# Constants fetched to one partition and spread by a matmul, with a new order table, in a fused attention and rational feed-forward kernel

## Chip, cores and metric

The kernel runs on one core of one Trainium2 chip. The metric is the device time of one launch in microseconds (us), the median of three runs: 771.01 us before the change (770.82 to 772.5).

## What is computed

Two small attentions in a row, then a feed-forward layer whose activation is a quotient of polynomials. B = 8 batches, H = 8 heads, 576 rows of 64, 32 packed rows; d_model 512, d_ff 2048. The weights w_in and w_out, a and b arrive as float64 words or float32 as the host gives them; the two weights are fetched as 64-bit words and turned into float32 on the chip.

```python
def sm_attn(qq, kk, vv):
    s = scale * np.matmul(qq, kk.transpose(0, 1, 3, 2))
    s = s - np.max(s, axis=-1, keepdims=True)
    a = np.exp(s)
    a = a / (np.sum(a, axis=-1, keepdims=True) + 1e-09)
    return np.matmul(a, vv)
p_packed = sm_attn(p, k, v)
out = sm_attn(q, p_packed, p_packed)
...
h = x @ w_in
P = a[0] + a[1] * h + a[2] * h2 + a[3] * h3
Q = 1.0 + np.abs(b[0]) * np.abs(h) + np.abs(b[1]) * h2
g = P / (Q + 1e-6)
return (g @ w_out).astype(np.float32)
```

## The kernel before

**How the work is cut.** The feed-forward layer is cut into 128 units (batch, half of its 576 rows, chunk of 256 of the 2048 columns), 16 to a batch (lines 976 to 980). A unit makes its h by matmuls into the PSUM banks h (TensorE, `hidden`, L902), reads it three times on ScalarE (Y, U and sq, lines 918 to 920), works on Y on VectorE (921, 922), adds U and sq on GpSimd, takes logarithm and exponential on ScalarE and finishes g on VectorE (929 to 941). Three units later `acc_block` (L983) multiplies g by the w_out chunk into the banks acc. The first 12 units are computed in plain float32; after them every operand is split in a high and a low part and three products stand for one.

**Ahead of the units** stands the attention of batch 0 (`attention`, L636): keys (tiles nat0 and nat1, and their last 64 rows in AH) are transposed by TensorE, scored against p, turned by softmax on ScalarE and VectorE and multiplied by v into ppT; then the queries (tile w3) are transposed, multiplied by ppT, and a second softmax on VectorE (lines 849 to 865) leaves AH, the left operand of every h of the batch. The attention of each later batch is fed in between the units.

**Weights.** `load_words` (L466) fetches a chunk of w_in or w_out (1 MB as 64-bit words, two DMAs of 512 KB); `convert` (L517) turns it into float32 with two passes on ScalarE, two on VectorE and an addition on VectorE or GpSimd. Sixteen chunks in all.

**Constants.** `constants` (L423) makes a tile zero on VectorE, fetches a and b by two DMAs that repeat them on all 128 partitions (tile ab, lines 425 and 426), scales them into abS (427), works out a square root in eleven small instructions on the tile root (432 to 443) and loads four of the scaled values into ScalarE's registers (444, 445), which the three reads of h use as scale.

**What sets the order.** No instruction is issued where it is written. `Planner` (L106) records every operation; `order` (L287) decodes the text ORDER into one permutation of all recorded operations, and `issue` (L303) hands them to the engines in that permutation. Each engine's queue is therefore fixed, and worked off in order: an instruction whose operand is late holds up all behind it. SyncE issues every DMA but two, and in the trace the ones it issues use eight semaphores in turn. The planner's own costs (COST, DMA_RATE, `transfer`, `replay`) set nothing at run time but one thing: `idle` (L1110) puts filler matmuls, ident times zero, issued at L310, where the planner sees TensorE empty.

```python
low, high = np.frombuffer(zlib.decompress(base64.b85decode(ORDER)), np.uint8).reshape(2, -1).astype(int)
order = (np.cumsum(low + 256 * high) % 2**16).tolist()
...
for i in self.order():
    engine, calls = self.ops[i]
```

In the views of the profile nearly all instructions carry line 313, where `issue` calls the engine, so tiles tell them apart, not lines.

Of the kernel before, what the change touches and what calls it, by code (L numbers as in the profile page):

```python
# [13 lines left out]
F32 = mybir.dt.float32  # L14
# [5 lines left out]
ALU = mybir.AluOpType  # L20
# [17 lines left out]
    "j^%sxFC96&svVfn@4DY1LWY9Ht)($bs(yIUz6E`9PpfSCYjE3{ir)Wv%o3*5%N@wntuGI^ezGzZZT;D!%Le>6?_c+MMaAdQhS7>O"
    "ZxPxbZz<?wiyT9Cccrhn{@SHRk=x&*gf23>^mI+Gw?=%WLG=0E?O88T@6NvSfV3L=D}%3W*s@=KwMmovqOf<T$o9dUORZlHuM3oj"
    "2144Z5qomq8-ILw+txQEs(UV7`S1VOxJP$R(bN;yefQmxQ0j&6EO3QN6CsmqbpB0$#k1esVaw`+mi*=&`Ip{0YfIx{HMq=4&8S`>"  # L40
    "+VQXjXFTF0PU^3G>vLbwl&=fQHvR7I9ZbDz>!+jAu8k+m-u+w7Z0yZYq91<fO%>E-gF0|2BoDl!Nab^xI(PWdx8-f8#R^g4sVC-+"
    "d2Ol{XM99R_sDiN9#8)Ck0nkmEjKMcQV79)?`Q12=Wn^`VnUtMDLqzZ;ZeIIqP_Ktidev<%Tc-VYjRnb%9iy0{h_RG)gf^qT;?{5"
    ";*GsaKO;u1l(W%tfypj9D-CUXUXu*1a7inVv|Wppg=^H^LA40ijT$pXqMORnnz{A6^97mDn!INZ@o&4u?cX~T+xk@H@<XCWccqd_"
    "DmnL}R5GSa;|cug&B^DU)F!jqtxxKn`lTT*e)9Jz(BM&K%Z`W~4-o|-6{Vi|1%by*5qj|tUcZ{t$ew*6@%%4{`~GO7rSG2EcHg_3"
    "-k@?C_s4fq5oMCZ-&*(4_q<R4w#-9N;FZR<ti79p4Zo`fvZHcL24GMpmBW(ku3rqK-ZVZH5504*RGHj)Z$&ahyta86w5N@#ggirQ"
    "0|x3^9Rz>=dS7iw7onc{&DbA)?UldsqCB3Ze*9|ORXe1Wdtv*L)2`CCV^#3LizL7goF{02KqbV~sk9bPhvlG1r7bDaW1+QiB2xI("
    "i|$vRt997DF%y8_NTKWxLiK4g1!z^dVxT%4%j&dFbx=mBq6KY|0=E_L+M^4IPESotJy;bd0JKr-HHXADYr!r^nw3KeOPF5Ksj?rt"
    "jrmd^UvV^DA8$NZ<~1w(OB@#KWlOy$mAdWSd(PJMr<Yv}mDV}0Et8&yaEU11`r$WDWJ>XbYTn71rM1Irj%r+$WW-SyYQLE__tn;Q"
    "j4c^%K`*XSLpGTj(v>RuAW)?q1$u7MtrVM8fw2nl07;CfEih<Sffx7Gc}gjd9UNDi8oct1+dh_)>Vsg>xTI$22^c_?0F5OWva35="
    "sH3xBpc?P2lbh4Sj@6!|zg){il1d|*2JKa31R!?PKWcU9g-80=^jV<(Y|4z-&AGhq$QpexUDIE4q}Blbv})gaA|6u%49|<F^$;+8"  # L50
    "u@Jd!z>pI4FOmj&mcsE(r-zqj<la(%baxd6Uo<PUgSsS{W5~g(G^0SCmIWh~;IV{s@~&ClDzACiDvuM$_pa~n3f7KVH4c+v$*Hj%"
    "nb58HJ6VWX(&=jdaK+6B%mG74M@A?((5CA(=pYl*lO5GzP{*8)bO2n?SVC)eD^yg!g=pTp;lSO8v&-67eOwV|M6}j>E4;bJVW%5h"
    "CF+k2Cm-$!RirW`M5HYa-IY1R$(H^^W`2}@Z?h~r7LjT7QfI-ATzhrH{)&6INmj};zNfYh*TdR(4fO0WgM3Wk0__uT4w8|(V0U$V"
    "$==FtjViMKvlU(L)%*29m6U>?A3UO+_pt@sF})>I?|ki{*@w!q{&M8Ij67mWr<LWG<_wv_4}PE=uwFCj!vFFIrDfge%W?}0&qlH9"
    "wE{ZW@V2+p%0fcjGaFW!caiHpqGif?f3JiPU5OA%${A7G<fEi0Qo)Qhr9n%N*}@d0k|tIMduLJTLu{-rh$7{;sp*^{sPD0n;5CPJ"
    "jL2(7X#rY5sRv}l<TF9Kpae(`R15<&Tmdy`X{#F`RIa=VTD7%zR&S^+q|=>6N!sw%TI=p_p3F<CV0^gqn|@DFF9O<{L=X&H(luvG"
    "%KF+4SX<AKLpm~Z`+iX!oLg|Y5n0uoRso>oI=A5TTt%v<E%zl_VGeCR+je%2=wkWE+>6a!^MXSQ(>P?QPgemPz8!qs%a5)o>C}ac"
    "pZqK1`eZd^OZ;$fd07ZK2?_oNwJ55AKYcGJ4eQXELJRu<jxF<CUFIPhM8ii`=8ml_6^&$NP%4Hu9=Uq#E}+7&XX7#CB=1Iz<bx*G"
    "1BV|k`v|R;moyDmKxYeF(Shk2WwL%=XYDY9A?i)pwKS-@D<N*VR2^#>>|c#s?CQK@p!!SSonI1h@14$@E_5~9uBzuT7fQ~T5LJFT"
# [36 lines left out]
    "eyTH=Kn8hX7jOnAvjw9Bl!<Xuc2WkXqQI3xhFf^?Sec6+j^~)Eij5m(VE{3vD9?&c!wC3-D;wMrj}Z_!#$y1!Uh-fyojR;`O{&<q"
    "h6ziZsRhSN4{jxi6_JsE#JJg897|48O!NFq@Dh?9#&=k;Blu+xN6du`z^n3jmhyzKs5rrRQo{&GPeExKH^uTNjK5IaxhW)65y7#A"
# [1066 lines left out]
```

## Time and profile before

| | |
|---|---|
| time, median of 3 runs | 771.01 us (770.82 to 772.5) |
| span of the profiled execution, first to last instruction | 770.6 us |
| median less span | 0.4 us |
| TensorE busy | 742.8 us, 96% of the span |
| VectorE busy | 683.9 us, 89% |
| ScalarE busy | 654.6 us, 85% |
| GpSimd busy | 470.5 us, 61% |
| moved by DMA | 56.04 MB |

Engines are named PE (matmul), PEld (weight load), DVE (VectorE), ACT (ScalarE), POOL (GpSimd) and SP (SyncE). A busy PE can hide waits, because matmuls are pipelined and their ends are modelled. The filler matmuls count as busy too.

### The profile page before, as it was taken

What the parts mean: (1) busy time and instruction counts of PE and PEld (TensorE: products, weight loads), DVE (VectorE), ACT (ScalarE), POOL (GpSimd) and SP (SyncE); (2) the same over time, 40 slices, a digit from 0 to 9 for tenths busy, and PEclk for the clock granted to TensorE, in tenths of its full rate; (3) what the DMA queues carried; (4) which work ended last, traced back from release to release, by engine and by line L of the source; (5) the groups of instructions that cost most, each with busy time, mean ns of one, the idle gap of its engine ahead of it and who ended that gap; (6) DMA issues with size and microseconds to landing.
All of it is one profiled execution on the core that took longest, in us unless ns stands there. A gap on an engine that the chain in (4) does not pass through costs nothing.

```text
span 770.6 us, 15197 instructions
## 1 busy us (share of the span) xinstructions
PE 742.8 (96%) x5440; PEld 572.8 (74%) x5440; DVE 683.9 (89%) x1290; ACT 654.6 (85%) x1465; POOL 470.5 (61%) x456
## 2 busy tenths in 40 slices
PE   1899999999999999999999999999999999999997
PEld 1665544688787887788788887778788887878886
DVE  4799999998998889998999889998999889989873
ACT  4799998999887898889887898889887898898973
POOL 1134468866685556756685556755686556866653
PEclk9999999999999999999999999999999999999999
DMA  9994630206501155024601165023801131000001
GB/s 283 301 344 163 188 47 1 86 29 70 90 1 55 46 69 90 1 87 57 103 1 55 46 68 92 2 86 42 117 1 55 42 56 37 1 29 1 27 2 42
DMA packets 152044, 56.04 MB, mean 73 GB/s; under 512 B 122144, under 2 KB 141344, under 8 KB 151968
## 3 DMA queue, kind: packets, MB, share of 16 engines
q1 hardware_dynamic: 151744, 54.81, 31.9%
q8 instruction: 43, 0.70, 0.4%
q14 instruction: 33, 0.27, 0.1%
q10 hardware_dynamic: 224, 0.26, 0.1%
HBM read 45.62 MB, written 9.44 MB: 71 GB/s over the span
## 4 chain that ended last, share of the span: by engine, by line
PE 81%; DVE 6%; DMA 5%; ACT 5%; SPq 1%; POOL 1%; issue 1%; DVEq 0%; POOLq 0%; ACTq 0%
PE acc L313 42%; PE h L313 24%; PE at L313 14%; DVE Y L313 3%; DMA m<-in_moe_w_in_dram 2%; DMA w<-in_q_dram 1%; SPq L313 1%; ACT Y L313 1%; ACT sq L313 1%; DMA out_dram<-half 1%; POOL gl L313 1%; ACT U L313 1%; DMA w<-in_moe_w_in_dram 1%; DVE small L313 1%; DVE V L313 1%
## 5 line engine op out<-in xcount | busy, mean ns | idle before, releaser
L313 PE MATMUL acc<-w,gh 128*128 128x512 f32 x732 | 238.5, 407 | 0.7 <-ACT half L313 0.3
L313 POOL TENSOR_TENSOR U<-U,sq 128x576 f32<-128x576 f32 x128 | 184.3, 1440 | 88.5 <-ACT U L313 38.6
L313 PE MATMUL h<-AH,m 128*128 128x288 f32 x1024 | 201.8, 314 | 2.7 <-DVE Y L313 2.4
L313 PEld LDWEIGHTS h<-AH,m 128*128 128x128 f32 x1024 | 161.4, 188 | 42.3 <-DVE Y L313 21.0
L313 POOL TENSOR_TENSOR gl<-Y,gh 128x512 fp32r<-128x512 f32 x116 | 150.3, 1296 | 48.5 <-ACT gh L313 19.0
L313 PEld LDWEIGHTS acc<-w,gh 128*128 128x128 f32 x732 | 132.0, 188 | 40.1 <-issue 10.2
L313 ACT ACTIVATE Y<-h,abS 128x288 f32<-128x288 f32 x256 | 127.0, 511 | 31.0 <-PE h L313 24.0
L313 PE MATMUL acc<-w,gl 128*128 128x512 f32 x382 | 148.5, 413 | 0.0
L313 DVE SCALAR_TENSOR_TENSOR Y<-Y,abS,V 128x576 f32<-128x576 f32 x128 | 103.0, 805 | 32.9 <-ACT V L313 32.4
L313 ACT ACTIVATE sq<-h 128x288 f32<-128x288 f32 x256 | 106.9, 419 | 27.7 <-PE h L313 16.0
L313 DVE TENSOR_TENSOR Y<-Y,h 128x288 f32<-128x288 f32 x256 | 110.9, 446 | 21.2 <-ACT sq L313 6.0
L313 DVE SCALAR_TENSOR_TENSOR Y<-Y,abS,h 128x288 f32<-128x288 f32 x256 | 125.7, 505 | 2.6
L313 ACT ACTIVATE U<-h 128x288 f32<-128x288 f32 x256 | 101.9, 422 | 8.2 <-DVE V L313 6.2
L313 ACT ACTIVATE V<-U,one 128x576 f32<-128x576 f32 x128 | 98.3, 768 | 6.6 <-DVE Y L313 4.1
L313 PE MATMUL h<-AL,m 128*128 128x288 f32 x448 | 97.9, 295 | 0.0
L313 DVE SCALAR_TENSOR_TENSOR V<-U,V 128x576 f32<-128x576 f32 x128 | 96.2, 752 | 0.0
L313 DVE SCALAR_TENSOR_TENSOR Y<-V,Y 128x576 f32<-128x576 f32 x116 | 87.0, 750 | 1.5
L313 PEld LDWEIGHTS acc<-w,gl 128*128 128x128 f32 x382 | 71.4, 188 | 21.3 <-issue 7.7
L313 ACT ACTIVATE V<-V 128x576 f32<-128x576 f32 x128 | 84.2, 658 | 1.1
L313 PE MATMUL acc<-half,gh 128*128 128x512 f32 x240 | 80.7, 411 | 0.0
L313 ACT CAST gh<-Y 128x512 fp32r<-128x512 f32 x116 | 73.6, 634 | 6.2 <-DVE Y L313 5.7
L313 PEld LDWEIGHTS h<-AL,m 128*128 128x128 f32 x448 | 72.8, 188 | 0.9
(146 smaller groups left out, 973.8 us busy)
## 6 DMA issues: line engine op xcount, KB each, us to landing
w<-in_moe_w_out_dram SPq DMA_DIRECT2D x16, 512.0 KB, 5.7
out_dram<-half SPq DMA_DIRECT2D x15, 512.0 KB, 3.0
nat<-in_k_dram SPq DMA_DIRECT2D x48, 144.0 KB, 3.9
nat<-in_q_dram SPq DMA_DIRECT2D x48, 144.0 KB, 4.3
nat<-in_v_dram SPq DMA_DIRECT2D x24, 256.0 KB, 3.2
m<-in_moe_w_in_dram SPq DMA_DIRECT2D x10, 512.0 KB, 7.6
w<-in_moe_w_in_dram SPq DMA_DIRECT2D x6, 512.0 KB, 8.6
nat<-in_k_dram SPq DMA_DIRECT2D x4, 512.0 KB, 6.6
```

The source lines that it names most:

```text
L313: getattr(getattr(self.nc, engine), name)(*args, **kwargs)
```

## The change

The constants come to one partition (tile row, two DMAs with one row each) and are spread to all 128 by a matmul of a row of ones with them, into the bank V, from which VectorE copies ab. Tile zero and the ones are made ahead of the planned part. The planner's costs are altered, and the order table is another one.

```diff
-    DMA_ISSUE, DMA_START, DMA_END = 420, 1400, 1200
-    DMA_RATE = 100.0, 190.0, 370.0
+    DMA_ISSUE, DMA_START, DMA_END = 420, 1500, 2000
+    DMA_RATES = (4096, 395.0), (2048, 345.0), (1024, 308.0), (512, 270.0), (256, 225.0), (0, 100.0)
...
         if engine == "vector" and name == "tensor_scalar":
             per /= 2
+            fixed += (self.columns(aps[0]) == 128) * 64
+        if engine == "vector" and name == "reciprocal" and self.columns(aps[0]) > 8:
+            fixed += 83
+        if engine == "scalar" and name == "activation" and aps[0].space == aps[1].space == PSUM:
+            fixed += 25
...
+    tc.nc.vector.tensor_scalar(zero, ident[:, 0:D], 0.0, None, ALU.mult)
+    ones, row = sb.tile([1, P], F32, name="ones"), sb.tile([1, 6], F32, name="row")
+    tc.nc.vector.memset(ones, 1.0)
...
     def constants():
-        nc.vector.tensor_scalar(zero, ident[:, 0:D], 0.0, None, ALU.mult)
-        nc.sync.dma_start(ab[:, 0:4], a.rearrange("(o n) -> o n", o=1).broadcast_to([P, 4]))
-        nc.sync.dma_start(ab[:, 4:6], b.rearrange("(o n) -> o n", o=1).broadcast_to([P, 2]))
+        nc.sync.dma_start(row[:, 0:4], a.rearrange("(o n) -> o n", o=1))
+        nc.sync.dma_start(row[:, 4:6], b.rearrange("(o n) -> o n", o=1))
+        t = V_ring.next()[:, 0, 0:6]
+        nc.tensor.matmul(t, ones, row, start=True, stop=True)
+        nc.vector.tensor_copy(ab, t)
```

The two order tables, decoded, differ in these places (m0 to m3 are the first four chunks of w_in; places count from 0 on each engine's own queue):

| queue | before | after |
|---|---|---|
| SP, the first 28 DMAs | m0, m0, m1, m1, last keys, m2, m2, p four times, keys nat0, keys nat1, last queries twice, m3, m3, last v twice, v, v, w_out, w_out, queries, queries, b, a, last keys of batch 1 | keys nat0, last queries, a, b, last keys, last queries, m1, m1, p, m0, p, p, p, m0, m2, m2, keys nat1, m3, m3, v, v, w_out, last v twice, w_out, queries, queries, last queries of batch 1 |
| SP, next | w_out into w2, w_out into w3 (after the queries), keys of batch 1 | w_out into w2, keys of batch 1, w_out into w3 |
| VectorE, the twelve instructions on abS and root (427 to 443 but the memset) | places 29 to 57, the last seven of them inside the second softmax | places 1 to 21 |
| ScalarE, first entry | conversion of m0 | register load from abS |
| TensorE, the first entries | 16 transposes of nat0 and nat1, then p and the last keys | transposes of nat0 mixed with the new matmul, the last keys and p, then those of nat1 |
| VectorE, last instruction but one or two of unit 0, 1, 2, ... 7 (L930) | 76, 88, 104, 114, 134, 145, 155, 167 | 72, 86, 104, 121, 135, 145, 153, 166 |
| ScalarE, exponential of unit 0, 1, ... 7 (L928) | 68, 80, 95, 108, 123, 136, 149, 166 | 64, 78, 94, 109, 124, 137, 149, 167 |

All bytes fetched up to the second transfer of the queries are the same in both: 16 DMAs of 512 KB, one of 128, four of 64 and four of 16, so 8640 KB (8.85 MB), and the constants after the change. On each engine the entries differ until what ran at 337 us in the trace before (SP 199 us, GpSimd 371 us); behind that the queues are the same.

## Rows read from the trace of the kernel before

**Rows 1.** The page: busy time of the matmul engine, DVE, ACT and POOL, and the busy share of PE in 40 slices of 19.3 us.
```profile
PE 742.8 (96%) x5440; PEld 572.8 (74%) x5440; DVE 683.9 (89%) x1290; ACT 654.6 (85%) x1465; POOL 470.5 (61%) x456
PE   1899999999999999999999999999999999999997
```

**Rows 2.** Busy time by stretch: the stretch and its length in us, then busy us and instructions of PE, PEld, DVE, ACT and POOL, the granted clock of PE, the share of the DMA engines' time and GB/s. The last row is the filler matmuls of L310 alone (PE and PEld), from 0 to 60 us.
```profile
0.00:16.00 16.00, 0.00 (x0) 0.00 (x0) 5.33 (x7) 7.05 (x7) 1.29 (x8) 1.00 0.90 280
16.00:32.00 16.00, 14.24 (x204) 11.60 (x204) 11.77 (x22) 12.34 (x25) 4.50 (x2) 1.00 1.06 315
32.00:44.00 12.00, 10.75 (x147) 7.33 (x147) 11.61 (x31) 8.45 (x18) 0.00 (x0) 1.00 0.90 292
44.00:60.00 16.00, 14.90 (x120) 10.12 (x121) 14.54 (x25) 15.94 (x34) 8.52 (x5) 1.00 1.07 351
60.00:90.00 30.00, 28.96 (x206) 15.72 (x205) 29.53 (x60) 29.03 (x60) 12.94 (x8) 1.00 0.49 165
90.00:110.00 20.00, 20.00 (x129) 10.46 (x127) 19.14 (x31) 19.90 (x45) 11.95 (x8) 1.00 0.55 96
110.00:250.00 140.00, 140.00 (x928) 102.87 (x928) 130.91 (x248) 121.70 (x269) 102.04 (x96) 1.00 0.24 46
250.00:338.00 88.00, 87.63 (x709) 69.78 (x703) 82.46 (x161) 78.05 (x182) 55.93 (x58) 1.00 0.30 52
338.00:740.00 402.00, 400.12 (x2891) 323.03 (x2890) 363.17 (x683) 348.44 (x804) 258.68 (x260) 1.00 0.26 47
740.00:771.00 31.00, 26.16 (x130) 21.88 (x128) 15.45 (x27) 13.66 (x30) 14.65 (x15) 1.00 0.08 26
...
0.00:60.00 60.00, 13.16 (x118) 10.15 (x118) 1.00 0.99 310
```

**Rows 3.** The chain of work that ended last, from 0 to 60 us: start, length, what. A DMA's piece goes from its issue to its landing.
```profile
4.28 10.09 DMA m<-in_moe_w_in_dram
...
21.64 10.22 DMA w<-in_q_dram
31.86 0.14 issue
```

**Rows 4.** What reads the constants: the tile root and its instructions (shortest, median and longest ns, first and last start in us), and of the tile ab how long DVE sat idle for its two DMAs and how long these took from issue to landing.
```profile
L313 DVE TENSOR_SCALAR root<-root x5: 112/149/266, 33.7 to 39.5; 128x1 int32<-128x1 int32 x3, 128x1 f32<-128x1 f32 x2
L313 DVE RECIPROCAL root<-root x2: 154/154/154, 38.7 to 42.0; 128x1 f32<-128x1 f32 x2
L313 DVE SCALAR_TENSOR_TENSOR root<-root x1: 213/213/213, 42.2 to 42.2; 128x1 f32<-128x1 f32 x1
L313 DVE TENSOR_SCALAR abS<-root x1: 155/155/155, 42.5 to 42.5; 128x1 f32<-128x1 f32 x1
...
  DMA ab<-in_moe_b_dram: 0.6, 1
  DMA ab<-in_moe_a_dram: 0.2, 1
...
DMA to landing us min/median/max: 8.1/9.1/10.1
```

**Rows 5.** DVE in order of time: start, length, instruction, and in brackets the idle time ahead of it and who ended it.
```profile
35.06 0.47 DVE L313 STREAM_TRANSPOSE kx<-at 128x288 f32<-128x288 f32 x1
...
38.69 0.15 DVE L313 RECIPROCAL root<-root 128x1 f32<-128x1 f32 x1
38.79 0.75 DVE L313 TENSOR_REDUCE small<-kx 128x18 f32<-128x576 f32 x1
39.46 0.27 DVE L313 TENSOR_SCALAR root<-root 128x1 f32<-128x1 f32 x1
39.64 0.17 DVE L313 TENSOR_SCALAR small<-small 128x18 f32<-128x18 f32 x1
...
43.32 1.43 DVE L313 STREAM_TRANSPOSE AH<-kx 128x576 f32<-128x576 f32 x2
...
48.88 0.45 DVE L313 TENSOR_TENSOR Y<-Y,h 128x288 f32<-128x288 f32 x1 [0.50 <-ACT Y L313]
51.45 1.14 DVE L313 TENSOR_SCALAR w<-w 128x1024 int32<-128x1024 int32 x1 [0.66 <-ACT win L313]
```

**Rows 6.** PE in order of time: the first transposes, the transposes of the last queries, the product of the queries with ppT, the first h and the first product with w_out.
```profile
16.40 1.09 PE L313 MATMUL at<-ident,nat 128*128 128x128 f32 x4 [16.40 <-DMA nat<-in_k_dram]
17.28 1.91 PE L313 MATMUL acc<-ident,nat 128*128 128x128 f32 x8
...
32.65 0.98 PE L313 MATMUL acc<-ident,w 128*128 128x128 f32 x7
...
34.03 0.71 PE L313 MATMUL at<-kx,ppT 64*32 64x288 f32 x16
...
44.15 2.21 PE L313 MATMUL h<-AH,m 128*128 128x288 f32 x8 [0.21 <-DVE AH L313]
...
59.19 2.74 PE L313 MATMUL acc<-w,gh 128*128 128x512 f32 x6
```

**Rows 7.** ACT: the copy that leaves ppT.
```profile
31.43 0.37 ACT L313 COPY ppT<-acc 128x256 f32<-128x256 f32 x1 [0.41 <-PE acc L313]
```

**Rows 8.** Who PE waited for between 90 and 740 us: us in total, times, longest.
```profile
PE h L313 <- DVE Y L313: 1.7, 3, 0.7
```

More of the change, by code (lines that the diff above doesn't have):

```diff
@@ L38 @@
[L38 to L47, printed above, removed]
@@ L98 @@
[L98 to L102 removed]
+    "c-rk*XP6u1wVtC@*Nob#Yo+bY+uYU-_ue43!A>9$0|^EjE+LSR<R&2y$n^z697r7OKp=roOaME?xL{)&_kz8)xA$FbkydR~M!n4a"
@@ new lines @@
+    "v@Sa{TArJGpZv&=cvo7LZ{|DYJ@0$YXFNv+BT@?Zbt$+w$*FDCLe5CB*aO36C_b=^_QRzqc<91sxBY!hLO2tiyn~jBfc$V%$-s+}"
+    "HM&>6zBl~RQ{f%QtJ07Z#^{%R8i)32KY32nQg&|dFS^P)tCBg%1*abWjf|!*OpWlq{k||=(s%D`;s~XRi|_rjM=o+d{x-N?cw^<Z"
+    "J1@6s79BC)`I0Kl_ezqycn(ka`u&@?=S1LpJGE&D;2|ZXbKthNPM)W}pRQ=F=zRFZF^xlC*I0dE?U%xd7arU;skio`FtO+z<4Zr9"
+    "Te@?RWWniAR=4)Rs@UrfKKyEG=x_I&&D#=e>@A9SY<j2uxF%dDgwny|b9lj%x6$+`YZJmly#IO>c~l`51qv>j?{4Gm(F%pZIXU#6"
+    ")qgh)t^H)}t$(7e2d5tVW@_K2kp<g(RAridYTA6?cK@yXkIiBK3|m30+dso_K0^ENTKVY#UajN37aJxQ{NAWHH>~b$(S<`3yUL8i"
@@ new lines @@
+    "u|ct=`mMEbQGfOBg{N1#k1e|DTX=Zh9j^??yqnyOb@PrliY>w~v^8^|S%2I<L)bTzSI<8r*z(5GJKsH=SWfTteDLDdJA}Vo{h0Yx"
+    "-Sk~5WqtQN`vraeFV~k-o&ra}GfV$P<+`o&|ElBV%-EwjTRP#sm!uQz&uo0+<B`bBwt8MpS5aHBFp&<*?tNz6Zb8N2X*T=9A1vR@"
+    "+dF8a1*><=?d_;1C>~j!R!Ewv+-Y}l=hh=l3gN8uUR+Bx{qoIxCk_way#&(20iBRX5<R>^%ly3|{G@p08*}e^?<Y@G?4N$5uHtW{"
+    "55Mo#YAM~N&Bt7m8&1w~DW^9l(-T{(=WkdU!mSOn9lnik2@}Nnza)xheL&Y=%zyXgw~Kj>#8mt=;e{Xnije90WRBOLcwoOTw@*#S"
+    "@A*r9t12=1gevjpg9oS$$5-qdR8xkKKqOkw+9F6Q6JQO5NedZLY3!=0Z6S*Au0QE9Ywc0OUm6LgMf4r-`4(Olr0R~El8MOujeV<j"
@@ new lines @@
+    "8?M&XPk3Gin%Io?GldJzQc6nHW>y&8Nx$Vkf0hj7MYNAT{Lr!Q{#1&G2);+|!e!Ktwi+g$O9^*A693K{DJrE;np?!hSKs-?eLE~I"
+    ")+e741r&n!mmXX$_o>1JX^g*nU#Pf&ugKrJ+6)kQbVo$}f#=7zd>H=w2K7$f?%yl=C*AgLidyoUTjHXxPkNS!N`ezE#Kf{4k4S9!"
+    "(cf+shy#^hRyEwxU9$c|aC})Ti%s)6j1H-zlK9K5jtakE0L1a%KDT@QkDnvDgxfZkhk4F;sp*c7x}EWLXJ;<>usf#PyhAEozeCei"
+    ">IRKx`*X>kKdtEd-D5h@<J<f$5p3I{4Q_iprjdXDuV-cfT>ag&!k&ven_vD>X!{o3o-0p-yQ&8V!}dFbgGPQ{Aefs7ntMK8E0ObL"
+    "aZykXbM`ytJoa))_i=Ojcd(@#zWY<Z@~LMviXQNmdRyjheMp<|?)-_z6bJIv2Xk~)8=f6pykWEI#b1x)XgBYub-0GMZg;1i*$kKO"
@@ L103 @@
+    "tWo1DB?|lJNfiD6m#BX$)IU+7=zmP3*sborkV0Wx$Ymvf9!GH5T{NdWIia9g>$1Yd>1eYCsjMPnvlsX1G#eJ#QxeTQp~@P4xCap&"
+    "$Ho;#I;&}+S?6h-6T+;zVm92|(<qvCI>fG??AdXg<5#Ym7{;33m}jnBv8S1{?szRfXDDVhHFVZ&HFjv6)dsOhWIXv{&>aU{<Di!z"
+    "zN`b??9()EP0@7L=`sBkn4>ZJE8?Fma2UqrOV)8fHW{-Sjpibbv6!n?jH7whNW(frW#ob80*4->Mb1fN)-e?KjDlInS$!sFSmicF"
+    "*(#4=Sq)S6*+y24bGu(`9I?$l72)XkI3340QOB~6gXpXQc%1)S$#xOL#-{_8Qy8~H{2xDA<Y)"
 )
@@ L186, in transfer @@
         size = mybir.dt.size(args[1].dtype)
-        run = 1
-        for step, n in reversed(args[1].ap):
-            if step != run:
-                break
-            run *= n
+        runs = []
+        for dims in (args[1].ap, args[0].ap[1:]):
+            run = 1
+            for step, n in reversed(dims):
+                if step != run:
+                    break
+                run *= n
+            runs.append(run * size)
         n = 1
@@ L194, in transfer @@
             n *= m
-        return n * size / self.DMA_RATE[(run * size >= 256) + (run * size >= 1024)]
+        return n * size / next(rate for least, rate in self.DMA_RATES if min(runs) >= least)
     def price(self, engine, calls):
```

125 lines of the change are left out of this document (65 added, 60 removed).

## The prediction

> **What bounds the kernel now.** I read the busy shares first. TensorE (PE) is busy 96% of the span and its 40 slices are full but for the first and the last [rows 1], so whatever the change does must show in the time in which PE has nothing useful to do. The table by stretch says where that is [rows 2]. PE is busy 0 of the first 16 us, 14.24 of the next 16, 10.75 of 12 and 14.90 of 16: 39.9 of 60 us. Of these, 13.2 us are fillers, so up to 60 us PE works for 26.7 us and loses 33.3. From 60 to 90 us it loses 1.0, from 90 to 740 us 2.3 us (0.37 between 250 and 338, 1.88 behind it), at the end 4.8. What the change can win lies ahead of 90 us, therefore, and every us won there is a us of the total only if PE's dense part starts that much earlier.
>
> Who holds PE up there? Three limits follow each other. Up to 32 us it is the transfers: the DMA engines are at 0.90 and 1.06 of their time while VectorE (DVE) is busy 5.33 of 16 and 11.77 of 16 us, and the chain that ended last goes through transfers to the landing of the last queries at 21.64 + 10.22 = 31.86 us [rows 3]. From 32 to 44 us it is DVE, 11.61 of 12 us: scores come at 34.03 + 0.71 = 34.7 us, DVE's second softmax runs from 35.06 to 43.32 + 1.43 = 44.75 us, and the first h follows at 44.15 us, beside the second half of the last transpose [rows 5, 6]. From 44 to 90 us DVE (44.1 of 46) and ScalarE (ACT, 45.0 of 46) are both full: the chunks are converted on the same engines that work on the units, and the first product with w_out comes at 59.19 us only [rows 2, 6]. From 90 us on it is PE.
>
> **The change part by part.** All terms are changes of the profiled execution, whose span is 770.6 us; the median of the runs is 771.0, so 0.4 us lie around the span, and I carry them along.
>
> *Keys ahead.* The first keys can be transposed at some 5 instead of 16 us. But the bytes up to the last queries are the same 8.85 MB in both orders. They landed within 31.9 us, and ppT, which the early keys serve, was ready at 31.43 + 0.37 = 31.8 us [rows 7], while the queries' own transposes, which land after it, run to 32.65 + 0.98 = 33.6 us [rows 6]. Keys that come earlier shorten a branch that the queries end anyway; moreover the second keys stand behind 4.0 MB in the new order, behind 3.87 MB in the old, so the first scores cannot start before them. Gain 0. Cover: the landing of the queries. If it were gone, the most to be had is ppT's lead on the product of the queries, 34.0 less 31.8 = 2.2 us.
>
> *The constants' way.* The two repeated fetches landed 8.1 and 10.1 us after their issue, behind the queries, and DVE sat idle 0.6 + 0.2 us for them [rows 4]. That idle time was not the limit: the conversion it held up ended before the scores came. Now they stand third and fourth on SyncE's queue, ahead of everything that they delay. Their price on the queries' landing is bounded by 0 and by what they took at the end of the queue, two landings 0.3 us apart behind 31.86 (22.06 + 10.1 and 24.38 + 8.1 give 32.2 and 32.5); with one row for 128 I take 0.1 in all. The added matmul and copy have no row; the nearest are a small instruction of DVE, 0.15 us [rows 4], and a transpose, 1.09 / 4 = 0.27 us [rows 6]. They fall where PE had no work and DVE a third of its time, so 0. ACT's queue now begins with a register load that waits for them, and the conversions behind it start later; ACT was busy 7.05 of the first 16 us, and the landings of the first chunks hold it up. 0, and 1 us at most.
>
> *Root out of the softmax.* Seven instructions of DVE on root and abS stood between 35.06 and 43.32 us, in the very chain that gives AH. By their durations [rows 4] they are 0.11, 0.15, 0.27, 2 x 0.154, 0.21 and 0.155: 1.2 us at most. But neighbours overlap: from a root instruction to the next one it is 38.69 to 38.79 and 39.46 to 39.64, so 0.10 and 0.18 us for durations of 0.15 and 0.27 [rows 5]. Six of the seven are nearer to the short one: 6 x 0.10 + 0.18 = 0.8 us. I take 0.8, and 0.2 more since the transpose that started at 35.06 can follow the scores of 34.7. AH comes 1.0 us earlier (0.6 to 1.5). What is late next is the conversion of w_out chunks, as before.
>
> *Order from 32 to 60 us.* The DMA share fell to 0.90 between 32 and 44 us, 1.07 behind it: 0.17 x 12 = 2 us of transfer time were lost where SyncE waited for the queries to be transposed before it could refill their tile. The new order puts 512 KB of keys ahead of that wait, so that the chunks behind land 1 to 2 us earlier. DVE waited 0.66 us for a conversion and 0.50 us for the first Y [rows 5]; against this ACT does one more pass of a conversion ahead of the first Y; the nearest row is such a pass on DVE, 1.14 us [rows 5]. So between +1.1 and -1.2, the two waits together; I take -0.4, as the lost transfers speak for the gain.
>
> *Order from 60 to 90 us.* By their places, the last DVE instructions of units 0 to 7 come 4, 2 and 0 places earlier, then 7 and 1 later, 0, then 2 and 1 earlier; one of the 60 in this stretch takes 29.53 / 60 = 0.49 us. Unit 0 gains 2 us, unit 3 loses 3.4, the mean over eight is nil. But a place is not all: the conversions are spread so that PE can begin its products sooner, as DVE has the first g four places earlier. I take -0.4, with bounds of -3.4 and +3.4.
>
> *Order from 90 to 338 us.* PE is full, so the best that another order can find is the visible 0.37 us; the worst is not to be read from the trace (first rival below). I take 0. Behind 338 us nothing differs.
>
> Sum: +0.1 - 1.0 - 0.4 - 0.4 = -1.7 us, so 771.0 - 1.7 = 769.3 us.
>
> **A rule of the Trainium skill.** The first transposes run 1.91 / 8 = 0.24 us apart, those of the queries 0.98 / 7 = 0.14, though the granted clock stands at 1.00, its 2.4 GHz level, throughout [rows 2, 6]. "TensorE: Matmul & The Clock Gate", What's actually happening, says that a PE that has been idle runs at half its clock until it has worked for a while. By that rule the change buys a second slow start, since PE rests between the first keys and the second. The sum by it: eight transposes and the scores at twice their time, about 8 x 0.1 + 1 = 1.8 us, all ahead of ppT and thus inside its 2.2 us; 0 on the total by both, but with 0.4 us to spare, and the third rival below without it.
>
> **The rivals.**
> 1. *The dense part pays: slower.* Between 90 and 338 us some half of PE's queue changes places, and PE works in order: a product put just ahead of its operand stops all behind it. For it speaks that PE's rare stops before are of this kind, h waiting for DVE's Y, up to 0.7 us each [rows 8], and that DVE has little slack there, 130.9 of 140 us busy. Against it: three such stops in 650 us. Price: 0.7 us each; it outweighs the gain from the third stop on, and from the fifth (5 x 0.7 - 1.7 = 1.8) the kernel is slower beyond doubt. Six give 4.2 - 1.7 = +2.5, 773.5 us.
> 2. *The start gives more.* ACT and DVE are only full from 44 us on because they idle ahead of it; if the new order lets units run while chunks land, part of the 33 us comes back: DVE's two waits whole (1.2), the idle 0.4 of its 12 us, the 2 us of lost transfers and unit 0's 2 us. 1.0 + 1.2 + 0.4 + 2.0 = 4.6, 766.4 us. For it: the first product came 59.19 - 44.15 = 15 us after the first h. Against: ACT is busy 15.94 of those 16 us, so work must go elsewhere and not merely move.
> 3. *Nothing comes through.* AH comes 1 us earlier, but unit 3's seven places, 3.4 us, or the slow start eat it before 90 us: 771.0 us. For it: DVE and ACT do the same work in both orders, and only 0.8 us of DVE's leaves the full stretch.
>
> **How the numbers follow.** The forecast, 768.3 to 770.3, gets 0.42; rival 1 0.16; rival 2 0.22; rival 3 0.20. A difference of 0.2%, 1.5 us, is about what a measurement of this kernel can tell from none: below 769.5 is faster, above 772.5 slower. Of the forecast's 0.42 some 0.26 lies below 769.5, with rival 2 0.48 faster; the other 0.16 and rival 3 make 0.36 same; rival 1 0.16 slower. Predicted is 769.3; the range takes in rival 2 whole and the nearer half of rival 1, 765.5 to 772.8.
>
> **What would show it.** In the changed kernel's profile: the last transfer of the queries lands at 31.5 to 32.5 us in the chain of waits (keys ahead: nothing); no root instruction of DVE behind 30 us, and AH's last transpose ends at 43.4 to 44.2 us; DMA share above 0.95 from 32 to 44 us; the first product with w_out before 58 us; PE busy at most 0.5 us less between 90 and 338 us. The prediction is wrong if AH does not come earlier, if PE's stops between 90 and 338 us sum to over 2 us, or if the first 90 us hold over 3 us more useful PE work than before.

## The result and the profile after

The changed kernel takes 775.38 us (median of five runs, 774.97 to 779.29) where the kernel before takes 771.04 (five runs, 770.82 to 772.5): a ratio of 1.0061, 95% interval 1.0041 to 1.0081. It is slower by 4.3 us. Forecast were 769.3 us, in a range of 765.5 to 772.8. Executions in the chip's slower state, 826 us and longer, are left out throughout.

The profiled execution of the changed kernel took 774.99 us with a span of 773.2, so 1.8 us lie around the span. In the runs that follow, the kernel before has 1.9 to 2.1 us there as well (770.88 us with a span of 769.0). The traced execution of before, with its span of 770.6, is therefore the one of 772.5 us and not one at the median, as the prediction took it. That is why the two traces differ by 2.6 us only.

The table by stretch of the changed kernel, columns as in [rows 2], the last stretch being 3 us longer:

```profile
0.00:16.00 16.00, 4.46 (x16) 3.04 (x16) 3.62 (x14) 6.61 (x10) 1.88 (x8) 1.00 0.87 282
16.00:32.00 16.00, 12.70 (x184) 8.97 (x184) 13.50 (x23) 12.02 (x22) 3.81 (x2) 1.00 0.93 297
32.00:44.00 12.00, 10.06 (x118) 7.21 (x118) 9.65 (x19) 6.71 (x14) 0.12 (x1) 0.86 0.77 266
44.00:60.00 16.00, 15.11 (x139) 10.43 (x140) 15.66 (x30) 15.84 (x33) 5.99 (x4) 1.00 1.05 341
60.00:90.00 30.00, 29.57 (x212) 16.59 (x212) 29.91 (x59) 29.48 (x64) 11.10 (x6) 1.00 0.49 174
90.00:110.00 20.00, 20.00 (x123) 9.92 (x122) 19.34 (x34) 19.70 (x43) 10.14 (x5) 1.00 0.58 119
110.00:250.00 140.00, 139.44 (x904) 101.32 (x904) 132.07 (x247) 122.06 (x269) 105.44 (x98) 1.00 0.19 42
250.00:338.00 88.00, 87.75 (x708) 68.91 (x707) 82.03 (x157) 77.60 (x182) 55.57 (x58) 1.00 0.25 52
338.00:740.00 402.00, 400.49 (x2891) 322.91 (x2890) 364.82 (x688) 348.61 (x802) 259.97 (x262) 1.00 0.22 48
740.00:774.00 34.00, 28.63 (x143) 24.05 (x141) 16.42 (x29) 16.17 (x36) 15.36 (x15) 0.97 0.08 24
```

The first keys give PE 4.46 us of work where it had none. From 32 to 44 us, however, PE falls from 10.75 to 10.06 us, its granted clock to 0.86, DVE from 11.61 to 9.65 and the DMA share from 0.90 to 0.77: where DVE was the limit, everything waits now. Between 110 and 338 us PE's idle time goes from 0.37 to 0.81 us, and its stops there and behind are what they were [rows 8]:

```profile
PE h L336 <- DVE Y L336: 1.6, 4, 0.7
```

The place is found on DVE, in order of time. The third line is the multiplication that makes the four factors F of the first softmax, the fourth its first reader:

```profile
28.35 1.23 DVE L336 SCALAR_TENSOR_TENSOR m<-m 128x1024 int32<-128x1024 int32 x1
...
29.68 0.17 DVE L336 RECIPROCAL small<-small 128x2 f32<-128x2 f32 x1
29.88 2.26 DVE L336 TENSOR_TENSOR small<-small 128x4 f32<-128x4 f32 x1
32.25 0.35 DVE L336 TENSOR_SCALAR small<-acc,small 128x128 f32<-128x128 f32 x1
...
38.91 0.85 DVE L336 STREAM_TRANSPOSE kx<-at 128x288 f32<-128x288 f32 x2 [1.63 <-PE at L336]
```

and beside it on POOL:

```profile
29.71 2.41 POOL L336 TENSOR_TENSOR win<-m,win 128x1024 int32<-128x1024 int32 x1 [12.19 <-DVE small L336]
```

An instruction of 4 columns takes 2.26 us and ends at 32.14, with the end of POOL's addition at 32.12. The median of the eight of this operation on the tile is 0.16 us. No view lists that as a wait: DVE counts as busy, and the time must be read from the length. PE had stopped meanwhile, for a transpose that needs what F scales:

```profile
30.09 0.71 PE L333 MATMUL h<-ident,zero 128*64 128x96 f32 x6
33.04 0.33 PE L336 MATMUL acc<-ident,small 128*128 128x128 f32 x1 [2.24 <-DVE small L336]
...
35.37 1.97 PE L336 MATMUL acc<-ident,w 128*128 128x128 f32 x8
...
37.99 0.72 PE L336 MATMUL at<-kx,ppT 64*32 64x288 f32 x16
```

It idles 2.24 us, and then it is slow, as the first microseconds behind it show (columns as above):

```profile
31.00:32.00 1.00, 0.00 (x0) 0.00 (x0) 1.00 (x1) 0.00 (x0) 1.00 (x1) 1.00 0.85 229
32.00:33.00 1.00, 0.00 (x0) 0.00 (x0) 0.84 (x3) 0.00 (x0) 0.12 (x1) 1.00 1.03 418
33.00:34.00 1.00, 0.96 (x9) 0.96 (x10) 0.56 (x2) 0.00 (x0) 0.00 (x0) 1.00 1.03 372
34.00:35.00 1.00, 1.00 (x9) 0.80 (x8) 0.97 (x4) 0.78 (x3) 0.00 (x0) 0.70 1.00 320
35.00:36.00 1.00, 1.00 (x6) 0.78 (x5) 1.00 (x1) 0.92 (x4) 0.00 (x0) 0.50 0.49 167
36.00:37.00 1.00, 1.00 (x7) 0.94 (x5) 0.96 (x2) 0.48 (x1) 0.00 (x0) 0.50 0.01 5
37.00:38.00 1.00, 1.00 (x8) 0.61 (x6) 0.28 (x1) 0.73 (x3) 0.00 (x0) 0.59 0.00 0
38.00:40.00 2.00, 1.60 (x43) 0.80 (x50) 1.09 (x3) 1.03 (x1) 0.00 (x0) 1.00 0.80 231
```

The clock stands at 0.50, its 1.2 GHz level, from 35 to 37 us. Eight transposes of the queries take 1.97 us where seven took 0.98 [rows 6]. ACT copies ppT at 34.70 and not at 31.43 us [rows 7], the scores begin at 37.99 and not at 34.03 [rows 6], and AH's last transpose ends at 47.73 + 0.78 = 48.51 us and not at 44.75 [rows 5]:

```profile
47.73 0.78 DVE L336 STREAM_TRANSPOSE AH<-kx 128x576 f32<-128x576 f32 x1
```

Because SyncE waits for the queries' transposes too (5.9 us in one piece), the DMA engines stand still between 36 and 38 us. In the two traces AH ends 3.8 us later, and what stands behind it is 1.2 us shorter (724.7 us from AH's end to the end of the span, 725.9 before): together the 2.6 us between the spans.

The kernel before had the same meeting, elsewhere. Its ScalarE made the second pass of the fourth chunk of w_in ahead of the exponentials, so POOL's addition ran from 25.94 us:

```profile
25.94 2.42 POOL L313 TENSOR_TENSOR win<-m,win 128x1024 int32<-128x1024 int32 x1 [7.86 <-DVE small L313]
```

and a multiplication of 4 columns was held by it, on DVE, until 28.38:

```profile
27.37 1.01 DVE L313 TENSOR_TENSOR small<-small 128x4 f32<-128x4 f32 x1 [1.30 <-ACT small L313]
28.42 0.16 DVE L313 SCALAR_TENSOR_TENSOR small<-small 128x2 f32<-128x2 f32 x1
```

Nothing shows that it cost anything there: the queries landed at 31.86 us only, and PE then still waited for them. The new table puts that pass of ScalarE behind the exponentials, and with it DVE's two passes and POOL's addition: 3.8 us later, onto F.

### The profile page after: what moved, and what is told of

Read it like the earlier page. It is cut to its first block, busy times and chain, and to the rows that moved or that the text cites. A ratio compares the mean times of both kernels' runs of the same rounds, so it can differ in the third digit from the quotient of the medians.

```text
span 773.2 us, 15194 instructions
## 1 busy us (share of the span) xinstructions
PE 748.2 (97%) x5428; PEld 573.4 (74%) x5428; DVE 687.0 (89%) x1292; ACT 654.8 (85%) x1465; POOL 469.4 (61%) x456
## 4 chain that ended last, share of the span: by engine, by line
PE 78%; DVE 10%; ACT 9%; issue 1%; DMA 1%; POOL 1%; SPq 0%; ACTq 0%; DVEq 0%; POOLq 0%
PE acc L336 41%; PE h L336 23%; PE at L336 14%; DVE Y L336 4%; DVE small L336 2%; ACT Y L336 1%; ACT sq L336 1%; ACT V L336 1%; DVE w L336 1%; ACT kx L336 1%; ACT w L336 1%; DVE kx L336 1%; ACT U L336 1%; ACT m L336 1%; DVE V L336 1%
## 5 line engine op out<-in xcount | busy, mean ns | idle before, releaser
L336 PE MATMUL acc<-w,gh 128*128 128x512 f32 x732 | 241.5, 407 | 0.4 <-ACT half L336 0.4
L336 PE MATMUL h<-AH,m 128*128 128x288 f32 x1024 | 210.6, 316 | 2.4 <-DVE Y L336 2.3
L336 PEld LDWEIGHTS h<-AH,m 128*128 128x128 f32 x1024 | 163.8, 188 | 43.8 <-DVE Y L336 20.9
L336 ACT ACTIVATE U<-h 128x288 f32<-128x288 f32 x256 | 103.7, 426 | 7.8 <-DVE V L336 4.3
L336 PE MATMUL h<-AL,m 128*128 128x288 f32 x448 | 100.4, 296 | 0.0
```

The lines of the kernel that those rows point to most:

```text
L336: getattr(getattr(self.nc, engine), name)(*args, **kwargs)
```

## The experiments

Two theories stood at first. **S**: POOL's addition holds DVE's first softmax, and the late start is the whole loss. **D**: the new order of the dense part costs PE 2 us between 100 and 340 us. For D spoke that, by the ends of the units (DVE's multiplication into V, one for each unit, counted through the trace), unit 14 ended 0.4 us and unit 22 2.8 us later than before. All runs are compared with the kernel before on the same chip.

**The constants alone.**

```diff
-        nc.sync.dma_start(ab[:, 0:4], a.rearrange("(o n) -> o n", o=1).broadcast_to([P, 4]))
+        nc.sync.dma_start(row[:, 0:4], a.rearrange("(o n) -> o n", o=1))
...
+        nc.tensor.matmul(t, ones, row, start=True, stop=True)
+        nc.vector.tensor_copy(ab, t)
```


> The kernel before with only the fetch of a and b changed (two transfers to one partition, the matmul and the copy; the order table of before, the two new operations put right ahead of the first reader of ab; planner rates of before). Theory D (the new order loses places in PE's queue between 100 and 340 us) and theory S (the late first softmax at 30 us costs the time): 770.6 to 771.5, as before. Theory C (the new constants cost about 1.4 us outside the span, since the changed kernel's time is 1.8 us above its span): 772.2 to 772.7, with a span of 770.3 to 770.9.

771.35 us, ratio 1.0001 (0.9992 to 1.0009), span 770.3 in the profiled run of 772.08. The constants cost nothing, C is out.

**The order alone.** The changed kernel with the lines of that diff the other way round.

> The changed kernel with a and b fetched as before (broadcast to all partitions, zero fill inside the planner), new table and new rates. Theories D and S: 774.8 to 775.6, the whole loss. Theory C: 773.6 to 774.2. That the early broadcast transfers hold up the first keys would show as first transposes later than 5.4 us and a time above 776.

774.46 us, 1.0043 (1.0030 to 1.0056). That is just below what D and S forecast, and above C's range. The order makes the loss; the interval overlaps that of the whole change, so nothing shows that the constants would have to explain.

The tables of six runs are put together from the two, each entry at its relative place (chunk numbers count from 0):

```diff
 e3   new table to the end of unit 6  | old
 e6   new table to 120 us             | old
 e7   table of e5 to 120 us           | old
 e8   old table to 69 us              | new
 e10  old table to 69 us | new to 160 us | old
 e11  new table to 160 us (with e9's edit) | old
```

**The new start with the old rest, and the addition moved a little.** For the second run, two entries of the table go behind the scaling of the first product (fs, tot and rec are the small steps that lead to F):

```diff
 VectorE  mul fs
-VectorE  pass 2 of chunk 3 (1.23 us)
 VectorE  tot, rec, F, scale, scale
+VectorE  pass 2 of chunk 3
+GpSimd   addition of chunk 3
```


> The changed kernel with the new table only up to the end of unit 6 (about 100 us), and everything after it in the relative order of the table of before. Theory D: 771 to 773, units 20 to 50 at most 1 us behind those of before. Theory S: 774.5 to 775.5, since the start with the multiplication stretched to 2.26 us is unchanged. Mixed: 773 to 774.

> The changed kernel with two operations of the fourth block's conversion (the 1.23 us VectorE pass and the 2.41 us GpSimd addition after it) put behind the scaling of the first product in the order; nothing else is moved. The multiplication of 4 columns then takes 0.16 to 0.2 us in place of 2.26, the scaled product is copied at 31 to 32 us and not at 34.7, the clock stays at 1.00 between 34 and 38 us. Theory S: 771 to 772.3. Theory D: 774.4 to 775.5, since units 4 to 6 ended no later than before already with the late start.

e3: 776.99 us, 1.0076 (1.0060 to 1.0092), worse than the changed kernel; D as stated is not seen. But its unit 7 comes 11.6 us after unit 6 (8.0 in e1): the cut costs in itself, presumably since work that the old rest takes as done was not. e4: 773.29 us, 1.0030 (1.0020 to 1.0040), 2.1 us won. Its traced execution, one of 777.37 us, shows why not more. DVE:

```profile
30.24 0.17 DVE L333 TENSOR_TENSOR small<-small 128x4 f32<-128x4 f32 x1
...
34.92 3.34 DVE L333 SCALAR_TENSOR_TENSOR w<-w 128x1024 int32<-128x1024 int32 x1
...
122.39 3.50 DVE L333 TENSOR_SCALAR small<-small 128x18 f32<-128x18 f32 x1
```

POOL:

```profile
34.40 2.77 POOL L333 TENSOR_TENSOR win<-m,win 128x1024 int32<-128x1024 int32 x1 [16.98 <-DVE one L333]
...
121.98 2.52 POOL L333 TENSOR_TENSOR w<-w,w 128x512 fp32r<-128x512 f32 x2
124.44 1.42 POOL L333 TENSOR_TENSOR U<-U,sq 128x576 f32<-128x576 f32 x1
```

F is free at 0.17 us, and the addition now holds a conversion (3.34 for 1.22 us), and behind it the second softmax. At 122 us an addition of 18 columns, which belongs to the second softmax of batch 1, waits 3.50 us through three instructions of POOL that follow each other without a gap.

**No addition on POOL there; the old rest; both; the old start.**

```diff
-        (nc.gpsimd if converted % 2 else nc.vector).tensor_add(dst.bitcast(I32), hi, di)
+        (nc.gpsimd if converted % 2 and converted != 3 else nc.vector).tensor_add(dst.bitcast(I32), hi, di)
```


> The changed kernel with the fourth block's addition (1024 columns of win) on VectorE, right behind the scaling of the first product, in place of GpSimd; the 1.23 us pass before it stays where the new table has it. No GpSimd operation then runs between 25 and 40 us, so no VectorE operation of the first softmax is held: the multiplication of 4 columns takes 0.16 to 0.2 us, the scaled product is copied at 31 to 32.5 us, the second softmax ends its last transpose at 44.5 to 46 us (48.5 in the changed kernel). Theory S (GpSimd holds VectorE's first softmax): 771 to 772.5, below the 773.3 of e4_pass_later, where the addition only met another operation. Theory D (the new order loses PE's time between 120 and 340 us): not below 773.3.

> The changed kernel with the new table up to about 120 us, at a place where the two tables have done the same work but for four operations, and the relative order of before behind it; the start with its 2.26 us is unchanged. Theory D: 772.3 to 773.3, PE's useful work between 120 and 340 us loses 6.3 to 6.9 us (8.9 in the changed kernel, 6.5 in e1_constants). Theory S: 774.8 to 775.6.

> e5_add_on_vector and e6_old_tail together. If S and D both hold and add up: 768.8 to 770.5, faster than the kernel before. If only one holds: that one's time, 771 to 773.3.

> The order of before (with the new constants) up to about 69 us, where the two tables differ by four operations, and the new table behind it, with the new rates of the planner. Theory D: 773 to 774, units 30 to 50 some 2 us behind those of e1_constants although units 0 to 4 are level. Theory S: 770.8 to 771.6.

e5: 771.31 us, 1.0008 (0.9997 to 1.0018): taking POOL off this place gives back 4.1 us, all of the loss. F takes 0.16 us, AH ends at 44.40 + 0.78 = 45.2. e8: 771.25 us, 1.0007 (0.9995 to 1.0018): the new order behind 69 us costs nothing that can be measured. D has fallen. e6 and e7 (777.68 and 775.81; 1.0085 and 1.0058) are worse than their parents by 2.3 and 4.5 us, though their cut, at 120 us, leaves only four operations that one table has done and the other not. In e6 ACT waits 6.3 us for PE's h between 100 and 150 us, 0.9 in the changed kernel; why a cut there costs so much is not settled. A cut can cost in itself, so e3, e6 and e7 say nothing for D; e8, which loses nothing by its cut, speaks against it.

**F on ScalarE, the old rest from 160 us, the root early.**

```diff
-            nc.vector.tensor_mul(xr(F), xr(f), two(rec))
+            for r in range(NG if bb == 0 else 0):
+                nc.scalar.mul(of(F, r), of(f, r), rec[:, r : r + 1])
```

and for e12, in the table of before:

```diff
+SyncE, TensorE, VectorE, ScalarE  transfers of a and b, matmul, copy, scaling of ab, the root's chain
 first keys, conversions, first softmax
 second softmax
-VectorE, ScalarE  the root's chain, between the softmax's instructions
```


> The changed kernel with the order untouched and GpSimd's 2.41 us addition left where it is; only the multiplication of 4 columns that was held is made on ScalarE (two instructions of 2 columns, about 0.2 us each) for batch 0. Theory S in its narrow form (the addition holds only such VectorE operations, and nothing else is wrong with the start): the addition runs from 29 to 32 us and beside it the scaling, which reads PSUM, starts by 30.7 us; the scaled product is copied at 31.5 to 32.5 us and the time is 770.5 to 771.7. Rival (the addition slows or blocks all of VectorE, or what matters is the 1.2 us pass ahead of it): scaling still after 32.1 us, 774 to 775.5.

> e8_old_head with the relative order of before again from about 160 us on (three or four operations differ there). In e8_old_head's trace units 4 to 16 end 1.3 to 2.6 us ahead of e1_constants and units 40 to 50 only 0.7 to 0.9. Theory D2 (the new table gains until 160 us and gives 1.4 us back between 160 and 340): 769.5 to 770.3. Theory S alone (the dense part's order is worth nothing, what looked like a loss is the other order of the same work): 770.8 to 771.6.

> e9_scalar_mul with the relative order of before from about 160 us on. D2: 1 to 1.4 us less than e9_scalar_mul, 769.3 to 770.3. S alone: the same as e9_scalar_mul within 0.5 us.

> The kernel before with the new constants, their transfers first of all and the whole chain of the root ahead of VectorE's first conversion, so that its eight VectorE and two ScalarE operations no longer lie among the second softmax; all else in the order of before. The prediction's term: 1.0 us (0.6 to 1.5) less, 770.0 to 770.5, and 8.7 us from the first stream transpose to the last (9.7 before). What the changed kernel's trace suggests (9.6 us there without the root: it only filled gaps): 0 to 0.3 us less, 770.8 to 771.4, 9.4 to 9.7 us.

e9: 772.51 us, 1.0015 (1.0005 to 1.0026). Most of the loss is gone though the addition stays where it is. It lies above the 771.7 us forecast at most and, by the ratios, 0.5 us above e5, which is not explained (the intervals overlap). Its trace shows the narrow form of S, POOL:

```profile
29.63 2.42 POOL L333 TENSOR_TENSOR win<-m,win 128x1024 int32<-128x1024 int32 x1 [12.22 <-DVE small L333]
```

and DVE beside it:

```profile
29.60 0.17 DVE L333 RECIPROCAL small<-small 128x2 f32<-128x2 f32 x1
30.20 0.35 DVE L333 TENSOR_SCALAR small<-acc,small 128x128 f32<-128x128 f32 x1 [0.42 <-ACT small L333]
30.58 0.35 DVE L333 SCALAR_TENSOR_TENSOR small<-acc,small 128x128 f32<-128x128 f32 x1
```

The scalings, which read acc in PSUM, run at 0.35 us in the midst of the addition. e10: 771.78, 1.0005 (0.9996 to 1.0015); e11: 772.16, 1.0013 (1.0002 to 1.0023): level with e8 and e9, and nothing shows of the 1 us and more that D2 forecast. e12: 771.30 us, 1.0002 (0.9993 to 1.0011), and DVE's second softmax without the root:

```profile
33.64 0.85 DVE L310 STREAM_TRANSPOSE kx<-at 128x288 f32<-128x288 f32 x2 [0.21 <-PE at L310]
...
40.08 0.75 DVE L310 TENSOR_REDUCE small<-kx 128x18 f32<-128x576 f32 x1 [0.16 <-ACT kx L310]
...
42.20 1.42 DVE L310 STREAM_TRANSPOSE AH<-kx 128x576 f32<-128x576 f32 x2
```

It lasts from 33.64 to 43.62, 10.0 us, longer than the 9.7 with it. Where the root stood, DVE now idles for ScalarE (0.16 us at 40.08) or for its own last result.

**The same meeting in the kernel before, TensorE kept busy, and the held additions left out.** e13 adds 18 fillers ahead of the waiting transpose; e14, e15 and e17 leave out the addition of 1e-9 to the second softmaxes' sums; e16 moves four entries of the table of before:

```diff
-ScalarE  pass 2 of chunk 3
 ScalarE  exp, exp, exp, exp, copy
+ScalarE  pass 2 of chunk 3
-VectorE  pass 1, pass 2 of chunk 3
-GpSimd   addition of chunk 3
 VectorE  sub f
+VectorE  pass 1 of chunk 3
 VectorE  mul fs
+VectorE  pass 2 of chunk 3
 VectorE  tot
+GpSimd   addition of chunk 3
 VectorE  rec, F, scale, scale
```

The edits of e13 and of the three without the addition:

```diff
-            todo = [("matmul", (first_sum if opened else first_h, z, words), dict(start=True, stop=True, skip_group_check=True))] * max(n, 0)
+            n = max(n, 0) + 18 * (i == 119)
+            todo = [("matmul", (first_sum if opened else first_h, z, words), dict(start=True, stop=True, skip_group_check=True))] * n
...
-            nc.vector.tensor_scalar(m2[:, 1, :], m2[:, 1, :], 1e-9, None, ALU.add)
```


> The changed kernel with 18 more filler products (about 0.12 us each) on TensorE ahead of the transpose that waits for the held multiplication; all else as in the changed kernel, the wait of 2.1 us included. If the lower clock behind the idle time costs its own share: the clock stays at 1.00 from 33 to 38 us, the eight transposes of the queries take 1.0 to 1.1 us and not 1.97, the second softmax ends about 1 us earlier (47.3 to 47.8 us) and the time is 774.0 to 774.7. If the clock costs nothing (the chain waits for VectorE anyway): 775.0 to 775.8.

> e5_add_on_vector without the 16 additions of 1e-9 to the sums of the second softmaxes (each sum is at least 1, so the addition of 1e-9 rounds away in float32: it is left out and changes nothing). If VectorE's held additions cost the dense part its 1.0 us: units 1 to 50 take 282.4 to 282.8 us (283.5 in e5_add_on_vector) and the time is 769.8 to 770.6. If it is TensorE's order: 283.3 to 283.6, 771.0 to 771.5.

> The kernel before without the same 16 additions. None of them was held for long in its trace (0.4 us at 306 us), so at most 0.5 us less: 770.5 to 771.2.

> The kernel before with nothing changed but the place of four operations of the fourth block's conversion: ScalarE's second pass behind the exponentials of the first softmax, VectorE's two passes and GpSimd's addition behind it, as in the new table. Theory S: the addition starts at 28 to 30 us, a small VectorE operation of the first softmax takes 2 us and more, the scaled product is copied at 33.5 us or later (31.4 before) and the time is 773 to 775.5. Rival (the order of before has slack there, since the queries land at 31.86 us): 771 to 772.

e16: 773.14 us, 1.0028 (1.0014 to 1.0042); eight of its executions lie at 771.5 to 773.5 us, three at 776.1 to 777.1. The old order has no slack for it either, though the price is smaller in the median, 2.2 us. DVE:

```profile
29.63 2.25 DVE L311 TENSOR_TENSOR small<-small 128x4 f32<-128x4 f32 x1
```

POOL:

```profile
29.46 2.40 POOL L311 TENSOR_TENSOR win<-m,win 128x1024 int32<-128x1024 int32 x1 [12.63 <-DVE small L311]
```

The traced execution, the slowest, of 777.09 us, idles PE for 2.12 us and has its clock at 0.50 from 33 to 38; AH ends at 49.66 us.

e13: 774.56 us, 1.0046 (1.0033 to 1.0059), from 774.19 to 775.02. F still takes 2.25 us, and PE:

```profile
31.04 3.68 PE L330 MATMUL h<-ident,zero 128*64 128x96 f32 x42
34.65 0.33 PE L333 MATMUL acc<-ident,small 128*128 128x128 f32 x1
...
36.75 1.09 PE L333 MATMUL acc<-ident,w 128*128 128x128 f32 x8
```

The fillers run 0.7 us past the scaling, the clock stays at 1.00 through 40 us, and eight transposes take 1.09 us. From F's end to AH's it is 48.76 - 33.07 = 15.7 us, 16.4 in the changed kernel. AH was expected to end earlier than there and does not, as F itself ends 0.9 us later in this trace. A plainer case is in e2: PE stops as long as in the changed kernel, and the clock does not fall:

```profile
33.55 0.33 PE L333 MATMUL acc<-ident,small 128*128 128x128 f32 x1 [2.24 <-DVE small L333]
...
35.65 1.09 PE L333 MATMUL acc<-ident,w 128*128 128x128 f32 x8
```

There it is 47.66 - 32.65 = 15.0 us. So of the 3.3 us by which AH ends later than in e5 (48.51 against 45.18) the lower clock has some 0.7 to 1.4. In the times, e2 (1.0043) and e13 (1.0046) lie 1.2 to 1.4 us below the changed kernel (1.0061), within the intervals.

e14: 770.90 us, 1.0001 (0.9989 to 1.0013); e15: 770.57 us, 0.9985 (0.9972 to 0.9998); the last run joins e14's edit to e8:

> e8_old_head (the order of before up to about 69 us, the new table behind it) without the 16 additions of 1e-9, as in e14_no_epsilon. If the new table's dense part was only spoiled by the held additions: 769.8 to 770.4, and below e15_before_no_epsilon. If the new order is worth nothing in itself: 770.4 to 771.0, level with e15_before_no_epsilon.

771.68 us, 1.0000 (0.9991 to 1.0009). By the ends of the units, unit 1 to unit 50 take 283.5 us in e5, 282.7 in e14, 282.6 in e1 and e15: by these traces the held additions of 18 columns were most of what the new dense part takes longer, as expected. In the time this does not come out: e14 is level with e5 and e17 is not below e15. e15, the kernel before without those additions, is the only one whose interval lies below 1, by 0.02% at its edge.

## Why the prediction was wrong

The forecast had the wrong sign. Term by term:

1. *Keys ahead, 0.* **This is the step that failed.** With POOL out of the way, the whole change is 0.6 us from the kernel before (e5: -0.2 to +1.4 us). But the step priced the advance of the keys only from above ("the most to be had is 2.2 us"), and nothing of what the keys displaced. The pass of ScalarE that went behind the exponentials issues two passes on DVE and an addition on POOL, and these were never placed in time. Their price was 4.1 us (775.38 less 771.31, and the same by the ratios). The 2.2 us that ppT had ahead of its product were no cover against lateness, because the last transposes of the queries stand behind ppT's own in PE's queue. Before, PE had waited for the queries no longer than this:

```profile
32.00 0.30 PE L313 MATMUL acc<-ident,w 128*128 128x128 f32 x1 [0.61 <-DMA w<-in_q_dram]
```

   In the changed kernel F ends at 32.14 us, 28.98 before: 2.1 us are the hold, 1.1 a later start, with a pass of DVE of 1.23 us now ahead of it. ppT again lies 2.9 us ahead of its product, 35.07 and 37.99 us, but the product begins 4.0 us later. The trace of before had given the sign, a small multiplication of 1.01 us beside an addition on POOL.
2. *The constants, +0.1.* Right: e1 puts them between -0.6 and +0.7 us.
3. *Root out of the softmax, -1.0.* Wrong: in the changed kernel the root's last instruction starts at 23.1 us, as meant, and e12, which moves only the root and its transfers, gains nothing over e1 (ratios 1.0002 and 1.0001). The 0.8 us were read from the spacing of DVE's starts, as if the next instruction would have started that much earlier. The changed kernel's second softmax takes 9.6 us without the root, 9.7 with it [rows 5], e12's 10.0. The root had stood in gaps of the chain.
4. *Order from 32 to 60 us, -0.4.* The lost transfer time grew, share 0.77, but by the hold: the queries' transposes stand behind the waiting transpose in PE's queue. Without the hold the share is as forecast, 1.02 in e5 and 0.95 in e9. What it is worth was not tested apart.
5. *Order from 60 to 90 us, -0.4.* The direction was right, and by the traces the gain behind AH was larger than forecast. The first product with w_out comes 58.37 - 48.51 = 9.9 us after AH, 14.4 before [rows 5, 6]:

```profile
58.37 1.13 PE L336 MATMUL acc<-w,gh 128*128 128x512 f32 x2
```

   Unit 1 ends 17.9 to 18.0 us after AH in the five traces with the order of before up to there (before, e1, e12, e15, e16), 15.3 to 15.7 us after it in seven of the eleven with the new start (the changed kernel, e4, e5, e7, e9, e13, e14). In the other four (e2, e3, e6, e11) it is 16.6 to 17.9 us, so something else sets it there, which was not tried. (The three traces cut at 69 us, e8, e10 and e17, have 17.6.) It is no gain of the total, as AH comes late even without the hold: at 45.2 to 45.4 us in e5, e9 and e14, at 43.4 to 44.8 in before, e1, e12 and e15.
6. *Order from 90 to 338 us, 0.* Right within 1 us. The first rival named the right side, but not the place or the mechanism: PE stops for Y four times, 1.6 us in all, three times and 1.7 us before.

The second slow start that was weighed did come. The clock column of the tables reads 1.00 in the first 32 us, but the lengths of the scores' rows do not bear that out, before and after the change:

```profile
20.99 0.40 PE L313 MATMUL acc<-kx,small 64*32 64x256 f32 x1
...
20.87 0.63 PE L336 MATMUL acc<-kx,small 64*32 64x256 f32 x1 [0.20 <-ACT kx L336]
```

These scores took 1.30 us from the first start to the last end before, 1.96 us after. That is 0.7 us and not the 1.8 of the estimate, since the transposes of the keys, 0.21 us apart where those of the queries are 0.14, ran at the slow pace in both orders. What it cost in the total is not shown; the 2.2 us of ppT were no cover for it. The second place was not foreseen: the clock fell behind the 2.24 us for which F's lateness stopped PE.

Of the signs named ahead, AH spoke most clearly, 3.8 us later in place of earlier, and the DMA share (0.77, above 0.95 was said). The first product came at 58.37 us, not before 58; the landing of the queries no longer stands in the chain of waits, DVE's tile small does. PE's idle time between 90 and 338 us grew by 0.44 us, within the 0.5 that were allowed. The last sign of being wrong came as well: without the fillers PE is busy for 58.7 of the first 90 us, 54.9 before. Part of these 3.8 us is the same work at a slower pace, and e5 has 61.3 us without being faster, so it told nothing of the total. In the second rival the sum of 4.6 us counts only one of the two times 2 us that it names.

What holds DVE's instruction is shown by what is not held. In the changed kernel's trace 11 instructions of the forms tensor_tensor, scalar_tensor_tensor and tensor_scalar with all operands in SBUF began when more than 0.4 us of an instruction of POOL were left. Seven, of 2 to 18 columns, took 0.57 to 2.26 us where others of their form take about 0.17, and ended within 0.04 us of POOL's end. Two of 1024 columns took 1.01 and 1.51 us, 0.69 otherwise, and ended 0.55 us after it. Two tensor_scalar of one column were not held. Of the instructions with an operand in PSUM 484 began so, and none was held; nor was any of 48 reductions, transposes and reciprocals on SBUF. The Trainium skill, "SBUF — State Buffer", Who interferes with whom, says that VectorE and GpSimd share one pair of ports, that an instruction of VectorE with two inputs in SBUF, or a tensor_scalar in a mode that uses both its ports, meets a GpSimd instruction that reads SBUF, and that the one that comes second waits to the end of the other. By that rule the wait is what is left of GpSimd's instruction, and 4 columns don't make it shorter; the trace agrees, with 2.24 us left when F began and 2.26 taken, and so do e9's readers of PSUM. The planner's own rule (shares, line 208 before the change) lets products of up to 8 columns pass, which the trace does not.

## To carry to other kernels

When an order moves a long GpSimd instruction, or one that leads to it on another engine, place it in time and look which VectorE instructions on SBUF fall beside it: here it cost one of 4 columns its whole rest, and no list of waits showed it. Look for the sign in the trace of before, an instruction several times as long as others of its form. And do not count a lead that the trace shows as cover while both branches stand in one engine's queue. Where the meeting falls on a chain, giving the small instruction to ScalarE (e9) or the long one to VectorE (e5) took all or most of the loss away here; e4's reordering only met the next one.

## What was not expected

A held instruction of VectorE did not slip in between instructions of GpSimd that follow each other: at 122 us of e4 it waited through three, 3.50 us for 0.17. TensorE's clock stood at 0.50 for two to five microseconds behind a stop of 2.24 us (the changed kernel) and 2.12 us (e16), but stayed at 1.00 behind the same 2.24 us in e2; 0.7 to 1.4 us hung on that. And one kernel's executions lie up to 5 us apart, perhaps by where such a meeting falls: e4's traced one took 777.37 us, 3.3 of them in that single hold, with a median of 773.29; the others were not traced.
